# One weight pair fewer is converted in the FFT filter, and the conversions are spread differently

## The chip, the cores and the metric

The kernel runs on one core of a Trainium2 chip. The time is the device time of one execution in microseconds (us), a median of three runs. Engines: TensorE (PE, with PEld for its weight loads), VectorE (DVE), ScalarE (ACT), GpSimd (POOL), and SyncE (SP), whose queue issues every DMA of this kernel.

## The reference, cut

```python
def reference(x, filt_r, filt_i, w_in, w_out, w2_in, w2_out):        # x: 2 x 3008 x 256
    X = np.fft.rfft(x, axis=1)
    y = np.fft.irfft(X * (filt_r + 1j * filt_i)[None], n=3008, axis=1).astype(np.float32)
    t = y.reshape(6016, 256)
    h = t @ w_in                        # 256 x 2048
    t = np.maximum(0.01 * h, h) @ w_out # 2048 x 256
    h = t @ w2_in
    r = np.maximum(h, 0.0)
    return (r * r) @ w2_out
```

## The kernel before

**Filter.** The 3008 points are split as 47 x 64. The work runs in 32 units, 16 blocks of 16 channels times two batches. Iteration s of the loop (L686) has, in this order on each engine: TensorE `stage_a` (first transform of unit s, tile `pa`), `stage_b` of unit s-1 (second transform, `px`), `stage_i` of unit s-3 (back, `zps`; one product for units in `SWAP`, two for the others) and, from s = 19 on, `stage_o` (eight matmul instructions, a block `pi` of the inverse transform of the first half of the channels); VectorE a transpose of `zps` into `zin` (unit s-4), a transpose of `pa` into `bin` (unit s), the sum of two products for some units, and the product `px` times `fr`; ScalarE a copy of `px` into `xc` (two half copies for units in `SWAP`), sign rows that multiply the loaded `fi` by signs (`sign_k`, three or four columns per iteration), and the copies of `pi`; GpSimd the product of `xc` and `fi` and some of the sums. VectorE's product of a unit starts behind ScalarE's copy of that unit.

Behind the loop come 16 `fill` calls (L749): four products of the inverse transform for the second half of the channels into one of four PSUM tiles, and a copy out, on VectorE for the numbers in `OUT_V` and on ScalarE for the rest. The first fills need the transposes `zin` of all units of a batch. Between the fills stand the steps of `macro_steps`, which split the first 1024 tokens into the operands of the products.

**MLPs.** Both MLPs are done in 96 steps: a step is one weight pair (256 of the 2048 hidden columns) for one block of up to 1024 tokens. Its eight blocks of 128 x 128 x 512 are done as seven products (Strassen), and each product is three matmuls, since every fp32 operand is held as a hi part and a lo part. `up(i, part)` writes four PSUM tiles `ph0` to `ph3`, of each of which there is one; `down(i, blk)` adds the output into `py0` to `py3`. TensorE's order in a step is: the products A11 (into `ph0`) and S2 (`ph1`), two matmul groups of `down` of the step before, S1 (`ph2`), A12 (`ph0`), S3 (`ph3`), four groups of `down`, A22 (`ph1`), S4 (`ph2`), two groups of `down`. VectorE does five sums per step from PSUM: v (`ph1` and ScalarE's copy `p1`), u (`ph3` + v), and h of the blocks (1,1) (`ph2` + u), (1,0) (`ph1` + u) and (0,1) (`ph2` + v). For each of the four blocks ScalarE then applies the activation twice (`g` in fp32 and `gp` as its rounded hi part) and GpSimd takes the difference, the lo part. Since there is one `ph1`, the next step's S2 waits until h (1,0) has been read from it.

**Weights.** The weights come as pairs of words of 64-bit numbers and are turned into fp32 hi and lo parts by the kernel, a pair p in two halves k: `w_in` (0) and `w_out` (1). `narrow_w` makes the steps: `size` (ScalarE, L209), `upper` (VectorE, two instructions, L213 and L214), `signed` (L217), `exp` (L222) and `low` (L228), all VectorE; `load` (the DMA of the next pair's raw words); `add` (L236); for k = 0 `sums` (four sums of 128 x 128, L241 to L244); `hi_i`, `hi_o` (ScalarE, L269) and `lo_i`, `lo_o` (L273). `add`, `sums` and `lo` are on VectorE where `ON_VECTOR` names them for the kind of the pair, else on GpSimd. Their buffers hold one or two pairs.

**Order.** Every engine does its instructions in the order in which the code emits them. Two clocks, F and M, emit the conversion steps: `begin` enters each step with its start plus its entry in a table (`NARROW_F`, `NARROW_1`), and `tick` emits what is due. F ticks four times per iteration of the filter's loop, once per fill, and on with M. M ticks eight times a step of the MLPs (`TM`): two ticks behind v, one before and one behind the block of u and h (1,1), two in part 2, one behind h (1,0), one behind h (0,1). Tick 0 of M is the first of step 0. In the kernel before, pairs 0 to 3 start at F ticks `STARTS` = -10, 34, 72 and 112, thus about units 0, 10, 20 and 30, and pairs 4 to 7 at M ticks `STARTS_1` = 0, 32, 48 and 64. Pair 3 is first used in step 3 and pair 4 in step 8, since the first visit of the first token block has pairs 0 to 3 only.

## Time and profile before

| | |
|---|---|
| median of three runs | 1124.01 us (1123.03 to 1125.35) |
| the profiled execution | 1125.17 us, of which the span from first to last instruction is 1123.4 us |
| TensorE busy | 1106.2 us, 98% of the span |
| VectorE, ScalarE, GpSimd busy | 640.2, 659.8, 755.1 us |
| mean granted TensorE clock | 0.995 |
| filter loop | up to about 112 us |
| fills | 114.65 to 129.02 us |
| MLPs | from 129.02 us on |

In the rows below, a timeline row gives start and duration in us, engine, line, operation, result tile and source tiles, shapes, and how many instructions were put together; in brackets is how long the engine had been idle, and what released it. Tile names stand without buffer numbers. The ends of pipelined matmuls are modelled. A step of the MLPs is found in TensorE's timeline by its `ph` and `py` groups.

### The profile page before, as it was taken

The numbers are of one execution on the slowest core, as the hardware profiler recorded it, in microseconds if no ns is written. First come the engines' busy times: TensorE is split into PE (matmuls) and PEld (weight loads), VectorE is DVE, ScalarE is ACT, GpSimd is POOL, SyncE is SP. The second block draws the span as 40 slices with busy tenths as digits, with TensorE's granted clock in tenths as the row PEclk, the third lists the DMA queues.
The fourth block names the chain that finished last, engine by engine and source line by source line (L and its number), as shares of the span: only waits on it lengthen the run. The fifth ranks groups of instructions, "written<-read, shape, count | busy, mean of one in ns | idle before, by whom it ended". The sixth has DMA issues, their size and how long they took to land.

```text
span 1123.4 us, 14254 instructions
## 1 busy us (share of the span) xinstructions
PE 1106.2 (98%) x4800; PEld 883.7 (79%) x4800; DVE 640.2 (57%) x873; ACT 659.8 (59%) x1210; POOL 755.1 (67%) x612
## 2 busy tenths in 40 slices
PE   7899999999999999999999999999999999999998
PEld 4466878888888888888888888888888888888887
DVE  6799878866756746746754644434435334334332
ACT  3865566555645645645656766656656556556654
POOL 4685698876866867767768877557547547547544
PEclk8999999999999999999999999999999999999999
DMA  8644622135131221221113220200200200200100
GB/s 232 192 152 131 247 80 76 57 120 162 70 111 38 79 84 38 82 81 38 63 53 115 87 89 1 74 1 1 76 1 1 73 1 1 73 1 1 38 1 35
DMA packets 35240, 80.14 MB, mean 71 GB/s; under 512 B 4544, under 2 KB 14880, under 8 KB 35040
## 3 DMA queue, kind: packets, MB, share of 16 engines
q1 hardware_dynamic: 35168, 79.25, 21.2%
q8 instruction: 37, 0.61, 0.2%
q14 instruction: 35, 0.29, 0.1%
HBM read 51.31 MB, written 27.92 MB: 71 GB/s over the span
## 4 chain that ended last, share of the span: by engine, by line
PE 91%; DVE 3%; POOL 2%; DMA 2%; issue 2%; ACT 1%; SPq 0%; DVEq 0%; POOLq 0%; ACTq 0%
PE py L469 46%; PE ph L368 40%; PE pi L635 2%; DMA xin<-in_x 1%; PE pa L577 1%; PE px L589 1%; PE zps L619 1%; DMA fi<-in_fi 1%; POOL gp L391 0%; DVE zin L628 0%; DVE bin L584 0%; PE zps L621 0%; POOL t L607 0%; DVE t L601 0%; POOL xs L333 0%
## 5 line engine op out<-in xcount | busy, mean ns | idle before, releaser
L391 POOL TENSOR_TENSOR gp<-g,gp 128x512 fp32r<-128x512 f32 (+1 forms) x384 | 506.6, 1324 | 313.1 <-ACT gp L390 98.3
L469 PE MATMUL py<-gp,wao 128*128 128x512 f32 (+1 forms) x1152 | 287.1, 390 | 0.6 <-POOL gp L391 0.6
L469 PE MATMUL py<-gp,wbo 128*128 128x512 f32 (+1 forms) x1152 | 286.6, 391 | 0.0
L469 PEld LDWEIGHTS py<-gp,wao 128*128 128x128 f32 x1152 | 215.9, 187 | 48.6 <-POOL gp L391 1.0
L368 PE MATMUL ph<-xop,wbi 128*128 128x512 f32 (+1 forms) x1008 | 253.9, 390 | 0.0
L368 PE MATMUL ph<-xop,wai 128*128 128x512 f32 (+1 forms) x1008 | 253.8, 391 | 0.0
L469 PEld LDWEIGHTS py<-gp,wbo 128*128 128x128 f32 x1152 | 216.0, 188 | 47.8 <-POOL gp L391 0.3
L368 PEld LDWEIGHTS ph<-xop,wbi 128*128 128x128 f32 x1008 | 189.0, 187 | 41.8
L368 PEld LDWEIGHTS ph<-xop,wai 128*128 128x128 f32 x1008 | 188.9, 188 | 41.6
L402 DVE TENSOR_TENSOR u<-ph,v 128x512 f32<-128x512 f32 (+1 forms) x96 | 65.2, 680 | 176.0 <-PE ph L368 176.0
L381 ACT ACTIVATE g<-h 128x512 f32<-128x512 f32 (+1 forms) x144 | 89.4, 621 | 103.5 <-DVE h L402 102.3
L389 ACT ACTIVATE g<-h 128x512 f32<-128x512 f32 (+1 forms) x144 | 89.2, 619 | 88.2 <-DVE h L398 87.6
L402 DVE TENSOR_TENSOR v<-ph,p 128x512 f32<-128x512 f32 (+1 forms) x96 | 65.0, 678 | 120.7 <-PE ph L368 117.6
L398 DVE CUSTOM_DVE_ANT_0 h<-ph,u 128x512 f32<-128x512 f32 (+1 forms) x96 | 65.2, 680 | 84.0 <-PE ph L368 82.2
L402 DVE TENSOR_TENSOR h<-ph,u 128x512 f32<-128x512 f32 (+1 forms) x96 | 65.1, 679 | 55.0 <-PE ph L368 52.3
L422 ACT ACTIVATE p<-ph 128x512 f32<-128x512 f32 (+1 forms) x96 | 56.2, 586 | 54.8 <-PE ph L368 54.8
L382 ACT ACTIVATE gp<-h 128x512 fp32r<-128x512 f32 (+1 forms) x144 | 87.7, 609 | 0.0
L390 ACT ACTIVATE gp<-h 128x512 fp32r<-128x512 f32 (+1 forms) x144 | 87.7, 609 | 0.0
L387 ACT ACTIVATE r<-ph 128x512 f32<-128x512 f32 (+1 forms) x48 | 28.1, 586 | 68.8 <-PE ph L368 68.7
L381 ACT ACTIVATE g<-ph 128x512 f32<-128x512 f32 (+1 forms) x48 | 28.2, 587 | 59.9 <-PE ph L368 59.9
L344 DVE TENSOR_TENSOR xop<-x,xop 128x512 fp32r<-128x512 f32 (+1 forms) x33 | 49.4, 1497 | 13.4 <-ACT xop L338 7.2
L607 POOL TENSOR_TENSOR t<-xc,fi 128x384 f32<-128x384 f32 x32 | 35.4, 1111 | 24.2 <-ACT xc L597 18.1
(197 smaller groups left out, 1048.2 us busy)
## 6 DMA issues: line engine op xcount, KB each, us to landing
wraw<-in_w SPq DMA_DIRECT2D x32, 512.0 KB
xin<-in_x SPq DMA_DIRECT2D x32, 160.0 KB
xt<-xo SPq DMA_DIRECT2D x26, 188.0 KB
yt<-o SPq DMA_DIRECT2D x16, 256.0 KB
x<-yt SPq DMA_DIRECT2D x4, 1024.0 KB
out<-o SPq DMA_DIRECT2D x16, 256.0 KB
w<-wi SPq DMA_DIRECT2D x8, 448.0 KB
wi<-w SPq DMA_DIRECT2D x8, 448.0 KB
```

The costliest lines, as they stand in the source:

```text
L344: eng.tensor_tensor(t[:, 1, :n], x_f32[v][name], t[:, 0, :n].bitcast(F32), ALU.subtract)
L368: nc.tensor.matmul(ph[:, :n], w[:, i, k], x[:, j, :n], start=(first and a == 0), stop=(a == 2), skip_group_check=True)
L381: nc.scalar.activation(g[:, :n], h[:, :n], AF.Prelu, alpha=0.01)
L382: nc.scalar.activation(t[:, 0, :n], h[:, :n], AF.Prelu, alpha=0.01)
L389: nc.scalar.activation(g[:, :n], h[:, :n], AF.Square)
L390: nc.scalar.activation(t[:, 0, :n], h[:, :n], AF.Square)
L391: nc.gpsimd.tensor_tensor(t[:, 1, :n], g[:, :n], t[:, 0, :n].bitcast(F32), ALU.subtract)
L398: nc.vector._custom_dve(dve_ops.TENSOR_ADD_SAT, out=t[:, :n], in0=ph[:, :n], in1=s[:, :n], s0=F32_MAX, s1=0.0)
L402: nc.vector.tensor_tensor(t[:, :n], ph[:, :n], s[:, :n], ALU.add)
L422: nc.scalar.activation(p1[:, :n], ph[0][:, :n], AF.Copy)
L469: nc.tensor.matmul(acc[c, t][:, :n], w[:, j, 2 * f + c], g[:, k, :n], start=(p == p0 and f == t and a == 0), stop=(p == p1 - 1 and f != t ...
L607: nc.gpsimd.tensor_tensor(t2, xc, fi_of(units[s][1], units[s][1] + 1), ALU.mult)
```

## The change

Three pairs, not four, start on the F clock: pair 0 as before, with the loads of pair 1's raw words moved from ticks 23 and 35 to 46 and 58; pair 1 at F tick 64, beside units 18 to 30, with a table of its own that gives about one step per unit; pair 2 at 128, so that it begins in the loop's last two iterations and goes on beside the fills. Pair 3 starts at M tick 0, where pair 4 stood; pairs 4 to 7 start at 28, 40, 52 and 64. For all pairs on the M clock `sums` goes from GpSimd to VectorE. Of the fills' copies, seven go from VectorE to ScalarE. The second half of `fi` is loaded in two parts (in units 6 and 11 instead of all in unit 7), and its sign rows are two sets of half the size, in units 9 to 16 and 17 to 24.

```diff
--- before.py
+++ after.py
@@ -44,24 +44,24 @@
 SWAP_V = (3, 16, 17, 18, 20, 21, 25, 26, 27, 29, 30)
 
 
-FI = ((2, 4, 2), (4, 8, 2), (8, 16, 7))
+FI = ((2, 4, 2), (4, 8, 2), (8, 12, 6), (12, 16, 11))
 SGN = (1, 2)
-SIGN = ((4, 8, 4, 4), (8, 16, 9, 3))
+SIGN = ((4, 8, 4, 4), (8, 12, 9, 3), (12, 16, 17, 3))
 
 
 
 H0 = 3
 DRAIN = (2, 2, 2, 2)
 FILLS = 13
-OUT_V = (0, 1, 2, 3, 4, 5, 6, 7, 9)
+OUT_V = (0, 2)
 
 FIN = (0, 0)
 
 
 
 TM = 8
-STARTS = (-10, 34, 72, 112)
-STARTS_1 = (0, 32, 48, 64)
+STARTS = (-10, 64, 128)
+STARTS_1 = (0, 28, 40, 52, 64)
 STARTS_2 = 96
 
 
@@ -69,9 +69,19 @@
 SAVE = dict(b11=2, t2=3, t1=4, b21=5, t3=6, t4=7, b22=8)
 AGAIN = dict(b11=-30, t2=-6, t1=-5, b21=-4, t3=-4, t4=-1, b22=0)
 
-NARROW_F = dict(
-    size0=8, upper0=10, signed0=12, exp0=14, low0=15, add0=18, size1=18, upper1=20, signed1=22, load0=23, sums=23,
-    exp1=26, low1=27, hi_i=30, lo_i=31, add1=32, load1=35, hi_o=38, lo_o=39,
+NARROW_F = (
+    dict(
+        size0=8, upper0=10, signed0=12, exp0=14, low0=15, add0=18, size1=18, upper1=20, signed1=22, sums=23, exp1=26,
+        low1=27, hi_i=30, lo_i=31, add1=32, hi_o=38, lo_o=39, load0=46, load1=58,
+    ),
+    dict(
+        size0=8, upper0=10, signed0=15, exp0=19, low0=23, add0=26, load0=27, sums=28, hi_i=30, size1=30, lo_i=31,
+        upper1=33, signed1=38, exp1=42, low1=46, load1=47, add1=50, hi_o=53, lo_o=55,
+    ),
+    dict(
+        size0=8, upper0=10, signed0=14, size1=14, exp0=16, low0=18, load0=19, add0=20, upper1=22, sums=23, signed1=24,
+        exp1=26, low1=28, add1=29, load1=29, hi_i=30, lo_i=31, hi_o=32, lo_o=34,
+    ),
 )
 NARROW_1 = dict(
     size0=0, upper0=7, signed0=8, exp0=9, low0=11, load0=11, add0=11, size1=12, sums=12, upper1=15, signed1=15, exp1=15,
@@ -96,9 +106,8 @@
 ON_VECTOR = dict(
     F0=(),
     F1=("add0", "lo_o"),
-    F2=("lo_o", "add1"),
-    F3=("add0", "lo_o", "add1"),
-    N1=("add1", "lo_o"),
+    F2=("add0", "lo_o", "add1"),
+    N1=("add1", "lo_o", "sums"),
     N2=(),
     S=("lo_o",),
     M=("lo_b11", "lo_b21", "lo_t2", "lo_t3", "lo_t4"),
@@ -682,7 +691,7 @@
         n = len(units)
         h0 = w0 = 0
         for k, t in enumerate(STARTS):
-            begin("F", narrow_w(0, k, f"F{k}"), NARROW_F, t)
+            begin("F", narrow_w(0, k, f"F{k}"), NARROW_F[k], t)
         for s in range(n + 4):
             if 2 <= s < n - 3:
                 load_x(s + 3)
@@ -769,8 +778,8 @@
                 begin("M", {"load": load_part}, {"load": (NP - HALF - 2) * TM}, t)
             else:
                 begin("M", macro_steps(v, "M"), MACRO, t)
-        for p in range(NWA, NP):
-            begin("M", narrow_w(0, p, "N1"), NARROW_1, STARTS_1[p - NWA])
+        for p in range(len(STARTS), NP):
+            begin("M", narrow_w(0, p, "N1"), NARROW_1, STARTS_1[p - len(STARTS)])
         for p in range(NP):
             begin("M", narrow_w(1, p, "N2"), NARROW_2, STARTS_2 + 4 * p * TM)
             begin("M", split_w(1, p, "S", {}), SPLIT_W, ((NM - 1) * NP + p) * TM + LATE[p])
```

VectorE at the end of the loop, from the second last iterations to the transpose of unit 30 (`zin10`, from `zps0`), before:

```order
L222 TENSOR_SCALAR wi32_1019<-wb__991 128x512
L601 TENSOR_TENSOR t1_1024<-px_1007,fr_886 128x384
L228 SCALAR_TENSOR_TENSOR wm_983<-wraw0_794,wi32_1019 128x512
L628 STREAM_TRANSPOSE zin10_679<-zps1_122 128x16x16x2
L614 TENSOR_TENSOR t1_1024<-t1_1024,t2_1039 128x384
L236 TENSOR_TENSOR wi32_1019<-wb__991,wm_983 128x512
L601 TENSOR_TENSOR t1_1048<-px_1033,fr_886 128x384
L213 TENSOR_SCALAR wm_1043<-wm_1043 128x512
L214 TENSOR_SCALAR wb__1064<-wm_1043 128x512
L628 STREAM_TRANSPOSE zin11_120<-zps2_123 128x16x16x2
L217 SCALAR_TENSOR_TENSOR wb__1064<-wraw1_893,wb__1064 128x512
L628 STREAM_TRANSPOSE zin10_679<-zps0_121 128x16x16x2
```

and now:

```order
L623 TENSOR_TENSOR t1_983<-t1_983,t2_999 128x384
L610 TENSOR_TENSOR t1_1007<-px_993,fr_875 128x384
L637 STREAM_TRANSPOSE zin10_659<-zps1_122 128x16x16x2
L623 TENSOR_TENSOR t1_1007<-t1_1007,t2_1021 128x384
L610 TENSOR_TENSOR t1_1027<-px_1015,fr_875 128x384
L637 STREAM_TRANSPOSE zin11_120<-zps2_123 128x16x16x2
L637 STREAM_TRANSPOSE zin10_659<-zps0_121 128x16x16x2
```

The six conversion instructions of pair 3 among the transposes, products and sums of units 28 to 31 are gone.

VectorE in step 5 of the MLPs, from h (1,1) on to the next step's u, before (the second half of pair 5 stands behind h (0,1)):

```order
L402 TENSOR_TENSOR h_1810<-ph2_1758,u_1808 128x512
L228 SCALAR_TENSOR_TENSOR wm_1683<-wraw0_1419,wi32_1782 128x512
L402 TENSOR_TENSOR h_1842<-ph1_1757,u_1808 128x512
L402 TENSOR_TENSOR h_1852<-ph2_1758,v_1773 128x512
L213 TENSOR_SCALAR wm_1827<-wm_1827 128x512
L214 TENSOR_SCALAR wb__1854<-wm_1827 128x512
L217 SCALAR_TENSOR_TENSOR wb__1854<-wraw1_1491,wb__1854 128x512
L222 TENSOR_SCALAR wo32_1858<-wb__1854 128x512
L402 TENSOR_TENSOR v_1883<-ph1_1867,p1_1873 128x512
L228 SCALAR_TENSOR_TENSOR wm_1827<-wraw1_1491,wo32_1858 128x512
L402 TENSOR_TENSOR u_1913<-ph3_1869,v_1883 128x512
```

and now, from h (1,1) to h (0,1):

```order
L411 TENSOR_TENSOR h_1813<-ph2_1756,u_1811 128x512
L222 TENSOR_SCALAR wm_1773<-wm_1773 128x512
L223 TENSOR_SCALAR wb__1820<-wm_1773 128x512
L226 SCALAR_TENSOR_TENSOR wb__1820<-wraw1_1482,wb__1820 128x512
L231 TENSOR_SCALAR wo32_1824<-wb__1820 128x512
L237 SCALAR_TENSOR_TENSOR wm_1773<-wraw1_1482,wo32_1824 128x512
L411 TENSOR_TENSOR h_1847<-ph1_1755,u_1811 128x512
L411 TENSOR_TENSOR h_1857<-ph2_1756,v_1771 128x512
```

Five conversion instructions of pair 4's second half stand between the two h's where one of pair 5 stood. In step 6, from u to h (1,0), VectorE now has:

```order
L411 TENSOR_TENSOR u_1914<-ph3_1872,v_1886 128x512
L411 TENSOR_TENSOR h_1916<-ph2_1871,u_1914 128x512
L237 SCALAR_TENSOR_TENSOR wm_1779<-wraw0_1745,wi32_1892 128x512
L250 TENSOR_TENSOR wi32_1892<-wi32_1892 128x128
L251 TENSOR_TENSOR wi32_1892<-wi32_1892 128x128
L252 TENSOR_TENSOR wi32_1892<-wi32_1892 128x128
L253 TENSOR_TENSOR wi32_1892<-wi32_1892 128x128
L411 TENSOR_TENSOR h_1950<-ph1_1870,u_1914 128x512
```

Pair 5's `low` and its four sums stand there, which were on GpSimd in the kernel before.

GpSimd in steps 5 and 6, before (a block's difference is `gp`, `add0` is L236, pair 5's `lo_i` is L273):

```order
L391 TENSOR_TENSOR gp_1813<-g_1812,gp_1813 128x512
L236 TENSOR_TENSOR wi32_1782<-wb__1747,wm_1683 128x512
L241 TENSOR_TENSOR wi32_1782<-wi32_1782 128x128
L242 TENSOR_TENSOR wi32_1782<-wi32_1782 128x128
L243 TENSOR_TENSOR wi32_1782<-wi32_1782 128x128
L244 TENSOR_TENSOR wi32_1782<-wi32_1782 128x128
L391 TENSOR_TENSOR gp_1845<-g_1844,gp_1845 128x512
L391 TENSOR_TENSOR gp_1876<-g_1875,gp_1876 128x512
L273 TENSOR_TENSOR wbi_1885<-wi32_1782,wbi_1885 128x896
```

and now (`lo_i` is L282, `add0` is L245):

```order
L282 TENSOR_TENSOR wbi_1832<-wi32_1715,wbi_1832 128x896
L400 TENSOR_TENSOR gp_1850<-g_1849,gp_1850 128x512
L400 TENSOR_TENSOR gp_1879<-g_1878,gp_1879 128x512
L400 TENSOR_TENSOR gp_1907<-g_1906,gp_1907 128x512
L400 TENSOR_TENSOR gp_1919<-g_1918,gp_1919 128x512
L245 TENSOR_TENSOR wi32_1892<-wb__1860,wm_1779 128x512
L400 TENSOR_TENSOR gp_1953<-g_1952,gp_1953 128x512
L400 TENSOR_TENSOR gp_1984<-g_1983,gp_1984 128x512
L282 TENSOR_TENSOR wbi_1993<-wi32_1892,wbi_1993 128x896
```

The four sums have left this queue; pair 4's `lo_i`, pair 5's `add0` and pair 5's `lo_i` follow each other at distances of four and two block differences.

## Rows read from the trace of the kernel before

**Rows 1.** The page: busy time and share of the span, engine by engine.

```profile
PE 1106.2 (98%) x4800; PEld 883.7 (79%) x4800; DVE 640.2 (57%) x873; ACT 659.8 (59%) x1210; POOL 755.1 (67%) x612
```

**Rows 2.** TensorE's timeline, units 12 to 19: start us, us, engine, line, operation, operands.

```profile
41.97 1.02 PE L577 MATMUL pa<-xin,ra 94*128 94x512 f32 x2
...
45.53 1.62 PE L589 MATMUL px<-bin,cb 128*128 128x384 f32 x2 [2.53 <-DVE bin L584]
...
57.07 1.02 PE L577 MATMUL pa<-xin,ra 94*128 94x512 f32 x2
...
59.87 1.02 PE L577 MATMUL pa<-xin,ra 94*128 94x512 f32 x2
...
62.66 1.02 PE L577 MATMUL pa<-xin,ra 94*128 94x512 f32 x2
...
64.81 1.02 PE L577 MATMUL pa<-xin,ra 94*128 94x512 f32 x2
```

**Rows 3.** Timelines of ScalarE and VectorE, units 9 and 10; brackets: idle before, releaser.

```profile
36.73 1.12 ACT L573 ACTIVATE fi<-fi,sg 128x64 f32<-128x64 f32 x3
...
38.40 1.62 ACT L573 ACTIVATE fi<-fi,sg 128x128 f32<-128x128 f32 x3 [0.56 <-DMA fi<-in_fi]
...
41.62 0.56 DVE L601 TENSOR_TENSOR t<-px,fr 128x384 f32<-128x384 f32 x1 [2.81 <-ACT xc L597]
```

**Rows 4.** TensorE's timeline, unit 20 to the first fills.

```profile
67.90 1.02 PE L577 MATMUL pa<-xin,ra 94*128 94x512 f32 x2
...
84.73 0.91 PE L589 MATMUL px<-bin,cb 128*128 128x384 f32 x2 [0.37 <-DVE bin L584]
...
107.38 2.04 PE L635 MATMUL pi<-dd,zin 128*128 128x128 f32 x16
...
114.65 14.37 PE L635 MATMUL pi<-dd,zin 128*128 128x128 f32 x120 [1.48 <-DVE zin L628]
```

**Rows 5.** ScalarE's timeline, copies of the last fills.

```profile
127.64 1.95 ACT L642 ACTIVATE xo<-pi 128x376 f32<-128x376 f32 x4
```

**Rows 6.** TensorE's timeline in the MLPs, first matmuls of two steps.

```profile
188.16 1.56 PE L368 MATMUL ph<-xop,wai 128*128 128x512 f32 x6
...
198.66 1.56 PE L368 MATMUL ph<-xop,wai 128*128 128x512 f32 x6
```

**Rows 7.** VectorE's timeline, the steps between them, and conversion steps elsewhere.

```profile
45.31 0.64 DVE L217 SCALAR_TENSOR_TENSOR wb__444<-wraw,wb__444 128x512 int32<-128x512 int32 x1
...
109.87 0.68 DVE L236 TENSOR_TENSOR wi<-wb__991,wm 128x512 f32<-128x512 f32 x1
...
193.98 0.69 DVE L402 TENSOR_TENSOR h<-ph,u 128x512 f32<-128x512 f32 x1
...
194.59 1.78 DVE L236 TENSOR_TENSOR wo<-wb__1854,wm 128x512 f32<-128x512 f32 x1
...
198.00 0.68 DVE L402 TENSOR_TENSOR h<-ph,u 128x512 f32<-128x512 f32 x1
...
199.20 0.41 DVE L213 TENSOR_SCALAR wm<-wm 128x512 f32<-128x512 f32 x1
```

**Rows 8.** GpSimd's timeline in the same steps.

```profile
188.17 0.53 POOL L241 TENSOR_TENSOR wi<-wi 128x128 f32<-128x128 f32 x1
...
193.70 2.13 POOL L273 TENSOR_TENSOR wbi<-wi,wbi 128x896 fp32r<-128x896 f32 x1
```

**Rows 9.** Timelines of VectorE, GpSimd and TensorE, steps 1 to 3.

```profile
141.11 0.69 DVE L402 TENSOR_TENSOR h<-ph,u 128x512 f32<-128x512 f32 x1
...
144.44 1.30 POOL L236 TENSOR_TENSOR wi<-wb__1346,wm 128x512 f32<-128x512 f32 x1
...
145.33 1.56 PE L368 MATMUL ph<-xop,wai 128*128 128x512 f32 x6
...
158.19 1.43 PE L469 MATMUL py<-gp,wao 128*128 128x512 f32 x5 [0.56 <-POOL gp L391]
```

## The prediction

> **What bounds the kernel now.** The first view is the page: TensorE is busy in 1106 of the 1123.4 us [rows 1]. What can shrink is only the stretch in which TensorE waits, and that is the filter, the first 130 us. The second view is TensorE's timeline there. Unit 19 follows unit 18 after 2.15 us and unit 18 follows 17 after 2.79, with nothing waiting; the difference is a second inverse product, which units outside `SWAP` have. From unit 19 on, with a block of the inverse transform added, a unit takes 3.09 us (64.81 to 67.90) [rows 2, 4]. Against this pace I read where units come late: from unit 12 (41.97) to unit 16 (57.07) it is 15.1 us for four units [rows 2]. The third view tells why: ScalarE waits for the second half of `fi`, VectorE's product waits 2.81 us behind ScalarE's sign rows [rows 3], and pair 1's conversion stands between VectorE's transposes. At the end of the loop the fills' matmuls start at 114.65, held by VectorE's last transposes (1.48 us of waiting shown) [rows 4]. From there on TensorE has no wait but one of 0.56 us at 158.19 [rows 9]: in the MLPs every microsecond that TensorE is made to wait is added to the time.
>
> **What is gained in the filter.** *Units 12 to 16*: three of the four iterations have one inverse product (2.15) and one has two (2.79), together 9.3 us; it took 15.1. The change takes pair 1's conversion away from here, halves each sign row, and loads `fi`'s second half in two parts, the first of them earlier. What remains on ScalarE is two half copies and three sign rows of 0.37 (1.12 for three [rows 3]), with the copies some 2.1 us a unit, just under TensorE's 2.15. So I take the whole **-5.8 us**; if ScalarE and the two late loads cost half of it, -3. *Units 19 to 31*: three short waits go (the first is the 0.37 at 84.73 [rows 4]; with what follows each, 1.1 us in all), since pair 1 is now spread over twelve units and pair 2 starts only behind them: **-1.1**, between 0 and -1.1. *End of the loop*: between its last `bin` and the transpose that frees the fills VectorE had twelve instructions, of which six convert pair 3; now it has the filter's six alone. TensorE's queue without waits: the sixteen matmuls at 107.38 take 1.9, an inverse product 0.65, a block 0.93 and another inverse product 0.65 (3.09 less 2.15 is the block), so the fills start at 111.5 instead of 114.65 [rows 4]: **-3.1**, at worst -1.5. Together **-10.0**, bounds -4.5 and -10.0.
>
> **What the fills and step 0 pay.** The fills are 14.37 us of TensorE [rows 4]. VectorE gives up seven copies and takes ten conversion steps of pair 2 (0.41 to 0.68 each if alone [rows 7]): about two us more. ScalarE takes the seven copies, 0.49 each (1.95 for four [rows 5]), and pair 2's four sums and one difference on GpSimd run between the operands' differences. Followed in queue order, the last fills come about 0.65 us late and `p1` of step 0 about 0.85 late, since pair 2's hi part now stands ahead of it on ScalarE: **+1.5**, between 0 and +3.
>
> **What the MLPs pay.** A step takes TensorE 10.5 us (188.16 to 198.66 [rows 6]). Count from its first matmul. VectorE's h of block (1,1) starts at 5.8 and ends at 6.5 [rows 7]; h of (1,0), 0.68 us, must end before the next step's second product, at 11.2, since that product overwrites the bank that h reads (before: it ended at 198.68, and the bank was wanted at 199.36 [rows 6, 7]). So between these two h's there are **4.0 us** for other work (the short gap); between the step's last h and the next step's u some 5 to 6.8, with v in it (the long gap). Before, the short gap held at most one or two conversion steps. What a step costs there is seen at 194.59: the sum `add1`, 0.68 at 109.87, took 1.78 us, because GpSimd's difference `wbi` ran from 193.70 to 195.83; it ended 0.54 us behind it [rows 7, 8]. The instructions that read PSUM stay at 0.69 all the while.
>
> The Trainium skill, SBUF — State Buffer, section "Who interferes with whom", has the rule: a VectorE instruction with two SBUF inputs, or in a two-port mode, and a GpSimd instruction that reads SBUF contend for one shared pair of ports, and the loser blocks for the whole instruction. By that rule, the trace agrees; if they shared instead, the waits below would all be the ones "in time", some 6 us.
>
> *Pair 3* (where pair 4 stood). Its four sums go from GpSimd to VectorE, into the short gap, and need GpSimd's `add0`, which stands behind block (1,1)'s difference. h of step 1 ends at 141.80, `add0` at 145.74 [rows 9]. No row has a 128x128 sum on VectorE; 128x512 takes 0.68 and GpSimd's 128x128 0.53 [rows 7, 8], so four take 0.7 to 2.1; I take 1.0, a quarter of 0.68 each and some waiting, as VectorE's own row is the nearest. h of (1,0) then ends at 147.4; TensorE wants its bank at 146.03 (145.33 [rows 9] and three products' matmuls of 0.23): +1.4. The next step's short gap, with `add1` and `lo_o`, loses 0.4, and the old wait of 0.56 goes: **+1.2**, 0.5 to 2.5.
>
> *Pairs 4 to 7* stood 16 ticks (21 us) apart, now 12 (15.75), and pairs 4 and 6 start in the middle of a step. That puts three kinds of work into the short gap:
> - Steps 5 and 8: upper, signed, exp and low of the second half, three at 0.41 and two at 0.64, 2.5 us alone. But GpSimd has block (1,1)'s difference (1.30, as `add0`) and the pair's `lo_i` (2.13) in the same time [rows 8, 9]. Played through with what 194.59 shows: 213 ends at 7.25, 214 at 7.7, 217 at 8.3, GpSimd's difference at 9.5, 222 at 9.75, `lo_i` at 11.75, 228 at 12.3, h at 12.95 against 11.2: +1.8 if the gap begins in time. It doesn't: the four sums and a copy ahead of it make h of (1,1) end near 8.9, and the wait becomes 3.4.
> - Steps 6 and 9: low, then the four sums behind `add0`. From h of (1,1) to `add0`'s end 3.9 us (141.80 to 145.74), sums 1.0, h 0.65: 5.5 us behind h of (1,1), at 12.0 if that is in time (+0.8); at 14.4 if it comes at 8.9, as it does behind seven conversion steps in the long gap, against a bank then wanted at 11.6 (+2.8).
> - Step 7: `add1`, upper, signed, `lo_o` and exp, 2.8 us alone, two of them behind GpSimd's differences: +0.7 in time, +2.2 late.
>
> In time everywhere: 2 x 1.8 + 2 x 0.8 + 0.7 = 5.9. Late: 2 x 3.4 + 2 x 2.8 + 2.2 = **+14.6**, and some eight smaller waits of 0.4 to 0.7 that I leave out, as each is the size of one meeting of two instructions more or less. I take the late sum, because the long gap is full too: a pair is 2 x 2.5 + 2 x 0.68 + 1.0 = 7.4 us on VectorE, and with six differences, `add0` and `lo_i` GpSimd has 7 x 1.30 + 2.13 = 11.2: 18.6 us of instructions that cannot run together, in 15.75. At 16 ticks it was 6.4 + 13.8 + 4 x 0.53, 22.3 in 21, and there rows are stretched already. With the smaller waits the upper bound is 19. In it is also this: the next pair's first raw half is loaded one tick ahead of its use on ScalarE, not five, and ScalarE's next block stands behind that wait.
>
> **The sum.** -10.0 + 1.5 + 1.2 + 14.6 = +7.3 us. The profiled execution took 1125.17 us (its span of 1123.4 and 1.8 around it); the median of three is 1124.01, 1.2 below. On the median: **1131.3 us**.
>
> **Rivals.** *The conversions fit* (faster). Where VectorE's instructions mostly miss GpSimd's, the short gap needs only their lone durations, 2.5, 2.8, or 1.6 and the wait for `add0`, in 4.0. Then the MLPs lose about 1 us beside the fills' 1.5, and the time is 1124.0 - 10.0 + 2.5 = 1116.5. For it: three pairs were converted in 180 to 240 us without one TensorE wait. Against it: the 1.78 of `add1`, and sums that have to wait for GpSimd in any case. It decides as soon as the MLPs' waits stay under 8.5 us. Chance 0.27.
> *Gain and loss cancel.* The gaps begin in time, pairs 3 to 7 cost 1.2 + 5.9 and the fills 1.5: 1124.0 - 10.0 + 8.6 = 1122.6, and 1124 with one late gap. Chance 0.13.
> *The clock falls as well.* Behind the 2.53 us wait at 45.53 two matmuls of px took 1.62 us where the pair otherwise takes half of that [rows 2]: TensorE ran at its lower level, 1.2 GHz, and lost some 1.8 us until it was back. Four or five waits of that length would do this again: 1124.0 - 10.0 + 2.7 + 19 + 4 x 1.8 = 1143. Chance 0.12.
> *The filter gives less.* ScalarE's sign rows or the late loads hold units 12 to 16, -4.5 instead of -10, with the MLPs' loss as forecast: 1137. Chance 0.06.
>
> **How the numbers follow.** The forecast has 0.42, its own range is 1125 to 1140. Within 0.2% is 1121.8 to 1126.3, about what a measurement of this kernel can tell from no change. Faster by more: the first rival and a little of the second, 0.29. Same: the rest of the second and the forecast's lower edge, 0.13. Slower: 0.58. The range goes from 1117, which leaves out the lower half of the first rival, to 1141, which leaves out the upper half of the clock's: together 0.2.
>
> **What would show it.** The fills' matmuls from 104.5 us on, unit 16 at 51.3. In the MLPs TensorE waiting for VectorE's `h` at the second product of steps 2 and 6 to 10, 1 to 3.5 us each; the four sums right behind GpSimd's `add0`; `low` of pairs 4 and 6 ending half a us behind GpSimd's `lo_i`. If TensorE has no waits in 140 to 240 us, the part on the MLPs is wrong; if the fills start behind 108, that on the filter.

## The result and the profile after

The changed kernel takes 1140.21 us (median of four, 1139.27 to 1140.66) against 1124.38 for the kernel before: a ratio of 1.0141, 95% interval 1.0123 to 1.0158. That is +15.8 us where +7.3 was forecast. The profiled execution took 1140.66 us, its span is 1138.9 us: 15.5 more than that of before.

The page of after, engine by engine (answers to [rows 1]):

```profile
PE 1106.3 (97%) x4800; PEld 881.7 (77%) x4800; DVE 648.9 (57%) x886; ACT 665.1 (58%) x1241; POOL 740.9 (65%) x592
```

TensorE's work is the same to 0.1 us. All that was lost is waiting, so the account can be read from TensorE's timeline, as the time between marks that both kernels have. Of after (starts of units 12, 16, 25, 26 and 31, the fills, and then step 0), answering to [rows 2, 4]:

```profile
41.23 1.02 PE L586 MATMUL pa<-xin,ra 94*128 94x512 f32 x2
...
50.48 1.02 PE L586 MATMUL pa<-xin,ra 94*128 94x512 f32 x2
...
77.46 1.12 PE L586 MATMUL pa<-xin,ra 94*128 94x512 f32 x2 [0.55 <-ACT xo L651]
80.16 0.91 PE L598 MATMUL px<-bin,cb 128*128 128x384 f32 x2 [1.57 <-DVE bin L593]
...
82.49 1.02 PE L586 MATMUL pa<-xin,ra 94*128 94x512 f32 x2
...
97.92 1.02 PE L586 MATMUL pa<-xin,ra 94*128 94x512 f32 x2
...
106.40 13.35 PE L644 MATMUL pi<-dd,zin 128*128 128x128 f32 x112
...
121.14 4.04 PE L377 MATMUL ph<-xop,wai 128*128 128x512 f32 x15
126.40 0.96 PE L377 MATMUL ph<-xop,wai 128*128 128x512 f32 x3 [1.21 <-DVE v L411]
```

The same timeline in the MLPs of after: the first matmuls of steps 2, 4, 5, 6, 7, 8, 9, 10, 11 and 12 and most of the stops between them, answering to [rows 6, 9]:

```profile
139.86 0.86 PE L377 MATMUL ph<-xop,wai 128*128 128x512 f32 x3
...
162.92 1.56 PE L377 MATMUL ph<-xop,wai 128*128 128x512 f32 x6
...
173.42 1.67 PE L377 MATMUL ph<-xop,wai 128*128 128x512 f32 x6
...
181.94 3.07 PE L478 MATMUL py<-gp,wao 128*128 128x512 f32 x12 [2.31 <-ACT o L504]
...
187.65 0.86 PE L377 MATMUL ph<-xop,wai 128*128 128x512 f32 x3
...
199.82 0.86 PE L377 MATMUL ph<-xop,wai 128*128 128x512 f32 x3
203.30 0.97 PE L377 MATMUL ph<-xop,wai 128*128 128x512 f32 x3 [2.62 <-DVE h L411]
...
213.97 0.86 PE L377 MATMUL ph<-xop,wbi 128*128 128x512 f32 x3
216.47 0.98 PE L377 MATMUL ph<-xop,wbi 128*128 128x512 f32 x3 [1.64 <-DVE h L411]
...
226.39 0.86 PE L377 MATMUL ph<-xop,wbi 128*128 128x512 f32 x3
230.64 0.96 PE L377 MATMUL ph<-xop,wbi 128*128 128x512 f32 x3 [3.39 <-DVE h L411]
...
240.90 0.86 PE L377 MATMUL ph<-xop,wbi 128*128 128x512 f32 x3
244.38 0.96 PE L377 MATMUL ph<-xop,wbi 128*128 128x512 f32 x3 [2.61 <-DVE h L411]
...
255.05 0.87 PE L377 MATMUL ph<-xop,wbi 128*128 128x512 f32 x3
...
266.53 1.56 PE L377 MATMUL ph<-xop,wbi 128*128 128x512 f32 x6
```

Three marks of before that its rows above don't have (unit 31, steps 4 and 12):

```profile
103.00 1.02 PE L577 MATMUL pa<-xin,ra 94*128 94x512 f32 x2
...
167.16 1.56 PE L368 MATMUL ph<-xop,wai 128*128 128x512 f32 x6
...
251.16 1.56 PE L368 MATMUL ph<-xop,wbi 128*128 128x512 f32 x6
```

| stretch of TensorE | before, us | after, us | change | forecast |
|---|---|---|---|---|
| up to unit 12 | 41.97 | 41.23 | -0.74 | 0 |
| units 12 to 16 | 15.10 | 9.25 | -5.85 | -5.8 |
| units 16 to 31 | 45.93 | 47.44 | +1.51 | -1.1 |
| unit 31 to the fills | 11.65 | 8.48 | -3.17 | -3.1 |
| fills to step 2 | 30.68 | 33.46 | +2.78 | +1.5 |
| steps 2 and 3 | 21.83 | 23.06 | +1.23 | +1.2 |
| steps 4 to 11 | 84.00 | 103.61 | +19.61 | +14.6 |
| from step 12 on | 872.2 | 872.4 | +0.1 | 0 |

So in these two executions the filter gave 8.25 us, and the fills and the MLPs lost 23.6. From step 12 on nothing is changed. The first row is noise, and a part of the second may be: in the traces of the runs below whose filter is that of after, unit 12 starts between 40.42 and 42.60 us, and units 12 to 16 take 9.25 or 9.26 each time; in those of the three runs whose filter is that of before (its sums moved, and the two with its starts alone moved) units 12 to 16 take 13.93 to 14.58, not 15.10.

The largest of TensorE's waits in the whole of after, by releaser (line and tile that waited, engine and tile waited for, us, times, longest):

```profile
PE ph L377 <- DVE h L411: 14.8, 11, 3.4
```

What VectorE did in these stops stands in its timeline of after: `add1` of pair 2 and v in step 0; h (1,1) of step 5 and the last three of the five conversion steps of pair 4 in the short gap of step 5 (the first two take 0.42 and 0.43); and pair 5's first sum:

```profile
123.10 2.64 DVE L245 TENSOR_TENSOR wo<-wb__1167,wm 128x512 f32<-128x512 f32 x1
125.66 0.68 DVE L411 TENSOR_TENSOR v<-ph,p 128x512 f32<-128x512 f32 x1
...
181.74 0.69 DVE L411 TENSOR_TENSOR h<-ph,u 128x512 f32<-128x512 f32 x1
...
183.26 1.68 DVE L226 SCALAR_TENSOR_TENSOR wb__1820<-wraw,wb__1820 128x512 int32<-128x512 int32 x1
184.97 1.41 DVE L231 TENSOR_SCALAR wo<-wb__1820 128x512 int32<-128x512 int32 x1
186.41 2.49 DVE L237 SCALAR_TENSOR_TENSOR wm<-wraw,wo 128x512 f32<-128x512 uint32 x1
...
201.50 0.29 DVE L250 TENSOR_TENSOR wi<-wi 128x128 f32<-128x128 f32 x1 [3.34 <-POOL wi L245]
```

GpSimd's timeline of after at the same places (pair 2's `lo_i`, two block differences, pair 4's `lo_i`, pair 5's `add0`):

```profile
123.07 2.13 POOL L282 TENSOR_TENSOR wai<-wi,wai 128x896 fp32r<-128x896 f32 x1 [0.55 <-ACT wai L278]
...
183.00 3.10 POOL L400 TENSOR_TENSOR gp<-g,gp 128x512 fp32r<-128x512 f32 x2 [3.48 <-ACT gp L391]
186.06 2.30 POOL L282 TENSOR_TENSOR wbi<-wi,wbi 128x896 fp32r<-128x896 f32 x1
...
200.19 1.27 POOL L245 TENSOR_TENSOR wi<-wb__1860,wm 128x512 f32<-128x512 f32 x1
```

`low` (L237) ends 0.54 us behind `lo_i`, at 188.90 and 188.36; the sum begins when `add0` ends, after 3.34 us in which VectorE does nothing. The Trainium skill, SBUF — State Buffer, section "Who interferes with whom", says that, where the two engines contend, whichever comes second waits for the whole instruction of the other. The trace agrees: L231, 0.43 where GpSimd is idle, took 1.41 here (to 186.38) and ended 0.28 us behind GpSimd's second difference (186.10).

### The profile page after: what moved, and what is told of

The parts are those of the page before. It is cut to its first block, busy times and chain, and to the rows that moved or that the text cites. A ratio compares the mean times of both kernels' runs of the same rounds, so it can differ in the third digit from the quotient of the medians.

```text
span 1138.9 us, 14294 instructions
## 1 busy us (share of the span) xinstructions
PE 1106.3 (97%) x4800; PEld 881.7 (77%) x4800; DVE 648.9 (57%) x886; ACT 665.1 (58%) x1241; POOL 740.9 (65%) x592
## 4 chain that ended last, share of the span: by engine, by line
PE 85%; DVE 7%; issue 4%; POOL 2%; DMA 2%; ACT 1%; SPq 0%; POOLq 0%; ACTq 0%; DVEq 0%
PE py L478 42%; PE ph L377 37%; PE pa L586 2%; PE zps L628 1%; PE px L598 1%; PE pi L644 1%; DVE h L411 1%; DMA xin<-in_x 1%; POOL wi L245 1%; DMA wraw<-in_w 1%; DVE wm L222 0%; PE zps L630 0%; POOL gp L400 0%; DVE u L411 0%; DVE wi L231 0%
```

## The experiments

All times are medians with the kernel before run beside them (1123.9 to 1125.0 us); "changed" is the changed kernel, 1140.2, beside which the kernel before took 1124.4.

### The four sums

Changed kernel, sums of pairs 3 to 7 back on GpSimd:

```diff
-    N1=("add1", "lo_o", "sums"),
+    N1=("add1", "lo_o"),
```

> The changed kernel with the four sums of pairs 3 to 7 on GpSimd again, as before the change; starts and tables as changed. Theory (the sums hold VectorE behind GpSimd's sum add0): the waits of 1.06 in step 2, 2.62 in step 7 and 2.61 in step 10 shrink by 1 to 2 us each, but GpSimd is busy 2.1 us longer per pair and VectorE's conversion steps meet it more often: 1133 to 1138. Rival A (sums are not what hurts): 1140. Rival B (GpSimd's added 2.1 us per pair block VectorE as much, and the low parts of the activations come late): 1141 to 1146.

Measured 1130.81 (1129.51 to 1133.83): 9.4 us less, below the theory's range. Moving the sums is the largest single part of the loss. The stops of 1.06, 1.05, 2.62 and 2.61 for `h` are gone; those of 2.31, 1.64 and 3.39 are now 2.46, 2.08 and 0.84, and one of 1.21 is new. TensorE's timeline of this run (the twelve `py` matmuls took 4.46 instead of 2.96, at a mean granted clock of 0.83 in 180 to 190 us):

```profile
181.51 4.46 PE L478 MATMUL py<-gp,wao 128*128 128x512 f32 x12 [2.46 <-ACT o L504]
```

Changed kernel, `add0` on VectorE too, so that the sums don't wait for GpSimd:

```diff
-    N1=("add1", "lo_o", "sums"),
+    N1=("add0", "add1", "lo_o", "sums"),
```

> The changed kernel with add0 of pairs 3 to 7 on VectorE too, so that the four sums no longer wait for GpSimd. Theory (the sums cost 9.4 us because VectorE stands still until GpSimd has done block (1,1)'s difference and add0: 3.34 us before the first sum at 201.50, 3.33 at 242.57): these standstills go, add0 takes 0.68 on VectorE, and the time is that with the sums on GpSimd or a little less, 1129 to 1132. Rival (VectorE and GpSimd exclude each other, so VectorE's own time counts, whoever is waited for): 1137 or more.

Measured 1134.55 (1133.86 to 1135.21), between the two: 5.7 of the 9.4 us come back, and theory and rival both fall. That the 5.7 were VectorE standing still behind `add0`, and the other 3.7 its own time, is not shown: the edit also takes `add0` off GpSimd and puts its 0.68 on VectorE.

Kernel before, with only this part of the change:

```diff
-    N1=("add1", "lo_o"),
+    N1=("add1", "lo_o", "sums"),
```

> The kernel before with one part of the change alone: the four sums of pairs 4 to 7 on VectorE instead of GpSimd; their starts stay 0, 32, 48, 64. Theory (a pair with its sums on VectorE holds TensorE at three second products and two other places, as in the run with starts 16 ticks apart, where two steps took 23.97 us instead of 21): 1.5 us for pair 4, as pair 3 cost in the changed kernel, and 3.0 us for each of the pairs 5, 6 and 7: 1124 + 10.5, about 1134. Rival (the sums hurt only where five pairs are squeezed in): 1124 to 1126.

Measured 1136.41 (ratio 1.0111, 1.0094 to 1.0128): +12.3 us, as the theory had it and a little more. The sums cost some 3 us a pair with four pairs and 16 or 32 ticks between them, so this is no matter of squeezing.

### Spacing, and starts in the middle of a step

Changed kernel, starts 16 ticks apart (sums still on VectorE), and the same with the sums on GpSimd:

```diff
-STARTS_1 = (0, 28, 40, 52, 64)
+STARTS_1 = (0, 16, 32, 48, 64)
```

> The changed kernel with pairs 3 to 7 started at M ticks 0, 16, 32, 48, 64 instead of 0, 28, 40, 52, 64, so 16 ticks (two steps, 21 us) apart and each at the head of a step. Theory (the 12-tick spacing and the mid-step starts cost the 19.6 us that steps 5 to 11 lost): raw words land five ticks ahead of their use, so the 2.31 us wait of TensorE for ScalarE's copy in step 5 goes; the waits of 3.39 and 2.61 at the second product go; what is left is the wait for the four sums, about 1 us per pair, and some waits in steps 2 to 4, where pair 4 now meets the operands of the second token block: 1140.2 - 19.6 + 5 + 2, about 1128. Rival (the four sums per pair that VectorE took over cost about 4 us a pair wherever it stands): 1138 or more.

> The changed kernel with the sums of pairs 3 to 7 on GpSimd and with starts 0, 16, 32, 48, 64. With both undone, steps 7 on are those of the kernel before. Theory (the sums and the dense, mid-step starts are two separate costs): the waits in steps 7 to 11 vanish; pair 4 now meets the operands of the second token block in steps 2 to 5, and costs 3 to 6 us there: 1140.2 - 19.6 - 1.2 + 3 to 6, so 1122 to 1126. Rival (sums are all of it, the spacing none): 1130.8, like the run with the sums alone.

Measured 1144.17 and 1128.57. The first theory fell: with the sums on VectorE the wider spacing makes it slower still. Two steps then take 23.98 us instead of 21, with three stops for `h` in each pair of them (0.91, 0.57 and 0.70 us); the starts of steps 8 and 10 in that run's TensorE timeline:

```profile
222.18 0.86 PE L377 MATMUL ph<-xop,wbi 128*128 128x512 f32 x3
...
246.16 0.87 PE L377 MATMUL ph<-xop,wbi 128*128 128x512 f32 x3
```

With the sums on GpSimd too, steps 6 to 11 take 10.5 us each as before, and the loss is in steps 4 and 5, which take 30.14 us instead of 21 (161.60 to 191.74). Pair 4 now stands there beside the splitting of the second token block: ahead of step 4's second product VectorE's `low`, then two operand differences (`xop`), take 1.71, 1.78 and 1.75 us between the two h's, beside GpSimd's own. The time, 1128.6, is above the theory's 1122 to 1126: in both places tried, a pair moved into the MLPs costs more than the filter gave.

Kernel before, starts alone: all three late pairs in the middle of a step, or 12 ticks apart (one of them in the middle of a step):

```diff
-STARTS_1 = (0, 32, 48, 64)
+STARTS_1 = (0, 28, 44, 60)
```

> The kernel before with pairs 5, 6 and 7 started at M ticks 28, 44 and 60 instead of 32, 48 and 64: still 16 ticks apart, but in the middle of a step. Theory (a mid-step start puts the five steps of the second half between the two h's, where they have 4.0 us and take 5.8): 1.8 us for each, 1129 to 1130. Rival (only the closer spacing costs): 1124 to 1125.

```diff
-STARTS_1 = (0, 32, 48, 64)
+STARTS_1 = (0, 40, 52, 64)
```

> The kernel before with pairs 5, 6 and 7 at M ticks 40, 52 and 64, so 12 ticks apart as in the change, one of them in the middle of a step; the sums stay on GpSimd. Theory (the mid-step start costs 1.8, the spacing another 1 to 2 a pair, as in the changed kernel with the sums on GpSimd, where steps 7 to 9 lost 5.5): 1127 to 1130. Rival (with the sums on GpSimd and only three pairs close together the gaps suffice): 1124 to 1125.

Measured 1135.54 (ratio 1.0090, 1.0075 to 1.0105) and 1132.24 (1.0057, 1.0042 to 1.0072). The mechanism stands and its price was too low twice over. The first run, TensorE in step 6:

```profile
187.12 0.86 PE L368 MATMUL ph<-xop,wai 128*128 128x512 f32 x3
190.37 0.97 PE L368 MATMUL ph<-xop,wai 128*128 128x512 f32 x3 [2.39 <-DVE h L402]
191.17 2.41 PE L469 MATMUL py<-gp,wao 128*128 128x512 f32 x6
193.38 2.99 PE L368 MATMUL ph<-xop,wai 128*128 128x512 f32 x9
```

GpSimd and VectorE in the short gap ahead of that stop:

```profile
183.75 3.18 POOL L391 TENSOR_TENSOR gp<-g,gp 128x512 fp32r<-128x512 f32 x2
...
187.25 2.46 DVE L228 SCALAR_TENSOR_TENSOR wm<-wraw,wo 128x512 f32<-128x512 uint32 x1
```

and the granted clock there (columns: stretch, its length, TensorE busy, clock, share of DMA, GB/s):

```profile
190.00:195.00 5.00, 4.63 (x13) 0.66 0.30 105
```

The stop is 2.39, not 1.8, since GpSimd has two block differences there (3.18 us), of which I had counted one; and behind the stop TensorE ran at its lower level for a while: six `py` matmuls took 2.41 instead of 1.56, nine `ph` 2.99 instead of 2.26, so that from step 6 to step 7 it is 14.69 us (187.12 to 201.81), 4.19 too many. The second run has two such stops (2.09 and 2.00), each in a step that takes 3.8 to 3.9 us too long.

### ScalarE's wait for raw words

In after ScalarE stands 2.86 us for pair 5's raw words, with the copy of an output tile behind it that TensorE needs (its timeline of after):

```profile
180.74 0.66 ACT L218 ACTIVATE wm<-wraw 128x512 f32<-128x512 f32 x1 [2.86 <-DMA wraw<-in_w]
181.31 0.58 ACT L504 ACTIVATE o<-py 128x512 f32<-128x512 f32 x1
```

Changed kernel with this step four ticks later, and the same with the sums on GpSimd:

```diff
-    size0=0, upper0=7, signed0=8, exp0=9, low0=11, load0=11, add0=11, size1=12, sums=12, upper1=15, signed1=15, exp1=15,
+    size0=4, upper0=7, signed0=8, exp0=9, low0=11, load0=11, add0=11, size1=12, sums=12, upper1=15, signed1=15, exp1=15,
```

> The changed kernel with the first ScalarE step of pairs 3 to 7 (size0) four ticks later, so that the raw words have five ticks to land. Theory (the 2.31 and 0.76 us waits of TensorE for ScalarE's output copy in step 5 come from ScalarE waiting 2.86 us for raw words): they go, and the time is 1137; the waits of steps 6 to 11 stay. Rival (with TensorE that much earlier, VectorE's sums are late by as much at the next second product): 1139.5 to 1140.5.

> The changed kernel with the sums on GpSimd and the first ScalarE step of pairs 3 to 7 four ticks later. With the sums on VectorE the later step gave nothing, as VectorE's output copy stood behind the sums instead. Theory (with the sums gone ScalarE's 3.00 us wait for raw words is what holds TensorE 2.46 and 0.76 us in step 5): these go, 1127.5 to 1128.5. Rival (VectorE's five conversion steps then meet GpSimd's differences as they did with the sums on VectorE): 1130 or more.

Measured 1141.24 and 1132.75: no gain in the one (against 1140.2), and none in the other (against 1130.8; the two intervals overlap). The rival was right in the second and nearly so in the first (1139.5 to 1140.5). TensorE's wait of 2.31 (2.46 in the other) is gone from the traces, that of 0.76 is not; VectorE's five steps and GpSimd's differences then meet in full: with the sums on GpSimd the next second product waits 2.39, and the clock falls to 0.66 in 189 to 194 us. So ScalarE's lateness had only hidden VectorE's.

### The filter

Kernel before with the split sign rows alone:

```diff
-SIGN = ((4, 8, 4, 4), (8, 16, 9, 3))
+SIGN = ((4, 8, 4, 4), (8, 12, 9, 3), (12, 16, 17, 3))
```

(with `FI` as in the change)

> The kernel before with one part of the change alone: the second half of fi loaded in two parts and its sign rows in two sets of half the size. Theory (units 12 to 16 were late by 5.8 us through ScalarE's long sign rows and pair 1's conversion together, the 2.53 us wait being behind the product that waits for ScalarE): about half of it goes, 1121. Rival A (the sign rows alone): 1118.3. Rival B (pair 1's conversion on VectorE alone): 1124.

Measured 1126.54 (ratio 1.0021, 1.0011 to 1.0031): rival B, or slightly worse. In its trace units 12 to 16 take 13.46 us (40.56 to 54.02): 1.64 less than in before, but only 0.47 less than in the fastest of the other traces of before's filter (13.93). Unit 16 alone then takes 4.45 us, 1.65 more than in before.

Kernel before with pairs 1 and 2 later, without and with the split signs:

```diff
-STARTS = (-10, 34, 72, 112)
+STARTS = (-10, 48, 80, 112)
```

> The kernel before with pairs 1 and 2 of the filter started later, at F ticks 48 and 80 instead of 34 and 72; pair 3 stays at 112. Theory (the 5.8 us of units 12 to 16 are pair 1's first half on VectorE beside units 12 to 15, where ScalarE's sign rows make products late; the signs alone gave nothing): they go, and pairs 1 and 2 stand where TensorE has a slower pace of 3.09 us a unit; some 1 to 3 us of new waits in units 17 to 28: 1119.5 to 1121.5. Rival (three pairs in units 14 to 31 hold TensorE for as long as they do now): 1123 to 1126.

> As the kernel before with pairs 1 and 2 later, and the sign rows split in two sets. Theory (with pair 1 gone from units 12 to 16, long sign rows on ScalarE are what is left there): 0 to 2 us faster than with the later pairs alone. Rival (the second set of sign rows, in units 17 to 24, meets pair 1 there): as much slower.

Measured 1126.42 (ratio 1.0019, 1.0007 to 1.0031) and 1126.89 (1.0029, 1.0019 to 1.0039): if anything slower, so the rivals. Units 12 to 16 do take 9.35 us then (41.78 to 51.13), so it is pair 1 that held them, not the sign rows; but the time comes back at once. TensorE's timeline of the first:

```profile
51.13 1.02 PE L577 MATMUL pa<-xin,ra 94*128 94x512 f32 x2
...
54.09 0.91 PE L589 MATMUL px<-bin,cb 128*128 128x384 f32 x2 [1.94 <-DVE bin L584]
...
105.31 1.02 PE L577 MATMUL pa<-xin,ra 94*128 94x512 f32 x2
```

Another stop of 1.79 stands at 68.67, and units 16 to 31 take 54.18 us where before they took 45.93; the fills start at 117.16. In the stretch from 60 to 90 us of before VectorE is busy 28.6 of 30 us: there is no room that a later start could find.

Four pairs in the filter with pairs 1 and 2 spread as the change spreads its pair 1, pair 3 where it has its pair 2, and the MLPs as before:

```diff
-STARTS = (-10, 64, 128)
+STARTS = (-10, 36, 82, 128)
-STARTS_1 = (0, 28, 40, 52, 64)
+STARTS_1 = (0, 32, 48, 64)
```

(the long table twice, pair 0's loads at 38 and 48, sums on GpSimd)

> Four pairs in the filter again and the MLPs as in the kernel before; but pairs 1 and 2 are spread over twelve units each by the changed kernel's table (starts 36 and 82) and pair 3 starts at 128, beside the loop's end and the fills; signs and copies as in the changed kernel. Theory (the filter's gain comes from having one pair fewer; a pair costs TensorE some 6 to 8 us wherever it stands in a filter in which VectorE is busy 28.6 of 30 us): 1121 to 1125. Rival (it comes from the even spread): the loop is as fast as the changed kernel's within 3 us and the MLPs lose nothing: 1116 to 1119.

Measured 1124.91, ratio 1.0000 (0.9990 to 1.0010). The theory: the filter's gain is that of one pair fewer, not that of a better spread. In its trace (an execution of 1123.15 us) units 12 to 31 take 61.45 us (39.65 to 101.10), against 61.03 in before and 56.69 in after.

Changed kernel (sums on GpSimd) with pair 1 one unit earlier, to part its `lo_i` from the first operand sum:

```diff
-STARTS = (-10, 64, 128)
+STARTS = (-10, 60, 128)
```

> The changed kernel with the sums of pairs 3 to 7 on GpSimd and pair 1 started four F ticks (one unit) earlier. Theory (the waits of 0.55 and 1.57 us in units 23 and 24 come from pair 1's lo_i on GpSimd, 2.44 us, standing with the first operand sum, 1.26 us, ahead of two units' products, while VectorE's size limits of the second half are stretched to 1.32 and 1.11 us beside them): apart from the operand sum, lo_i costs less, and 1.0 to 1.5 us come back: 1129.3 to 1129.8. Rival (pair 1 costs this wherever it stands in the loop): 1130.8.

Measured 1132.56 against 1130.81: no gain. The stops of 0.55 and 1.57 (in iteration 25 of the loop, at the first transform of unit 25 and the second of unit 24, not in units 23 and 24 as the expectation has it) became 0.66 and 1.58 one unit earlier. What they come from is not settled beyond this: they move with pair 1.

### The fills

Changed kernel (sums on GpSimd) with seven copies back on VectorE:

```diff
-OUT_V = (0, 2)
+OUT_V = (0, 1, 2, 3, 4, 5, 6, 7, 9)
```

> The changed kernel with the sums on GpSimd and seven of the fills' copies back on VectorE, as before the change. Theory (in the fills VectorE is the late engine: add1 of pair 2 ends at 125.7 and v of step 0 behind it, which makes TensorE wait 1.21 us): VectorE takes 7 x 0.55 us more, and step 0 is late by up to that: 1130.8 + 3, about 1133 to 1135. Rival (the copies go into VectorE's gaps, and ScalarE is freed): 1129 to 1131.

Measured 1133.46 (1131.07 to 1137.64) against 1130.81 (1129.51 to 1133.83): +2.7, in the theory's range, but the four times of each overlap and so do their intervals against the kernel before (1.0063 to 1.0126; 1.0040 to 1.0072). That moving the copies was worth doing beside a pair is likely and not shown.

Kernel before with pair 3 moved to tick 128 by the change's last table, and the copies moved:

```diff
-STARTS = (-10, 34, 72, 112)
+STARTS = (-10, 34, 72, 128)
```

> The kernel before with pair 3 at F tick 128 by the table that the changed kernel has for its pair 2, and the fills' copies moved to ScalarE as in the change; everything else as before. It shows the loop's end and the fills alone. Theory: the fills start 3.1 us earlier (-3.1), and fills and steps 0 and 1 pay 2.8, as in the changed kernel: 1123.5 to 1124.5. Rival (the fills' cost in the changed kernel came from pair 3 standing behind them in the MLPs): 1121 to 1122.

Measured 1123.73, ratio 0.9987 (0.9978 to 0.9997). In its trace unit 31 to the fills is 8.49 us (-3.16) and the fills to step 2 33.44 (+2.76): the two terms of the changed kernel once more, and they cancel.

That kernel and the four-pair one with the pair's last steps behind v of step 0:

```diff
-        exp1=26, low1=28, add1=29, load1=29, hi_i=30, lo_i=31, hi_o=32, lo_o=34,
+        exp1=26, low1=28, load1=29, hi_i=33, lo_i=34, add1=36, hi_o=37, lo_o=38,
```

> The kernel with pair 3 in the fills, with that pair's last steps later: hi_i and lo_i at 33 and 34 instead of 30 and 31, add1 at 36 instead of 29, hi_o and lo_o at 37 and 38, so behind v of step 0. Theory (v waits for add1, which takes 2.63 us beside GpSimd's lo_i, and p1 stands behind hi_i): TensorE's waits of 1.20 for v and of 0.24 go, and as the pair is wanted only in step 3 nothing takes their place: 1122.0 to 1122.7. Rival (add1, now between step 0's h's, holds the next second product for as long): 1123.5 to 1124.5.

> The four-pair kernel with the even spread, with the same later steps of pair 3. Theory: 1.2 to 1.7 us less than the 1124.9 of that kernel: 1123.2 to 1123.7. Rival: 1124.5 to 1125.5.

Measured 1126.13 (ratio 1.0014, 1.0003 to 1.0024) and 1127.94 (1.0020, 1.0007 to 1.0033): both beyond their rivals' ranges. The first is slower than without (0.9978 to 0.9997 there); the second is not clear of it (0.9990 to 1.0010 there), and its profiled execution, 1123.31, is the fastest of its twelve, so its trace does not show what made the median. The wait for v is gone from both traces, so the moved steps made it. In the first two others took its place; its TensorE timeline:

```profile
134.15 2.36 PE L382 MATMUL ph<-xop,wai 128*128 128x512 f32 x9 [1.92 <-DVE h L416]
...
156.93 1.98 PE L483 MATMUL py<-gp,wao 128*128 128x512 f32 x5 [2.34 <-POOL gp L405]
```

No kernel tried is faster than the kernel before by 0.2%; the best is the one with pair 3 in the fills, by 0.13%.

## Why the prediction was wrong

**What failed.** Of the 8.2 us between the forecast and the two spans, 5.0 are the MLPs' late sum (14.6, measured 19.61), 2.6 the units 16 to 31 (-1.1, measured +1.51) and 1.3 the fills (+1.5, measured +2.78); 0.74 ahead of unit 12 goes the other way. In the MLPs the mechanism was right and the sum too small, since eight small waits were put at nothing and step 5 was priced too low; in the filter and the fills waits came that the forecast did not have.

**Right.** The sign; which engine is waited for, and at which instruction; units 12 to 16 (-5.85 for -5.8), the loop's end (-3.17 for -3.1) and pair 3 (+1.23 for +1.2). The stops at the second products of steps 2 and 6 to 10 are there, with 1.05 to 3.39 us. Not every detail held: `low` of pair 4 ends half a us behind `lo_i`, that of pair 6 does not (it runs 0.69 us alone, and `exp` ahead of it was the one held). For units 12 to 16 the reason was half wrong: the sign rows had no part in it that the runs could show, pair 1 had all. And that -5.8 was met so exactly is in part luck: against the other traces of before's filter (13.93 to 14.58) the gain is 4.7 to 5.3.

**Steps 4 to 11: +19.61 for +14.6.** Step by step, by their starts in after, beyond 10.5 us each: 3.73, 1.67, 3.65, 1.92, 4.01, 3.65 and 0.98 for steps 5 to 11. Two parts of the working were too small.

First, the "eight smaller waits of 0.4 to 0.7 that I leave out". Where the forecast had 2.8, 2.2, 3.4 and 2.8 for the late h of steps 6, 7, 8 and 9, the second products came 2.8, 1.8, 3.6 and 2.8 us late (203.30, 216.47, 230.64 and 244.38, each less its step's start and the 0.70 of one product). What is over in steps 7 to 11 is 3.3 us in smaller stops. Leaving them out, as I did, treated them as if some could be less than nothing, and nothing in the gaps could make them so.

Second, step 5 and its h: 5.4 us (3.73 and 1.67) for 3.4. The working has "GpSimd has block (1,1)'s difference (1.30, as `add0`) and the pair's `lo_i` (2.13) in the same time". There were two differences, 3.10 us in after and 3.18 with the mid-step starts alone. The working has the five steps in 5.8 us (6.5 to 12.3); they took 6.55 (182.35 to 188.90), so some 0.75 of the 2.0 missing can be the second difference's; for the rest the cause stays open. That h of (1,1) would end near 8.9 was right (9.0: 182.43 less 173.42). More than half of the 5.4 (0.76 and 2.31 us) shows up as TensorE waiting for ScalarE's output copy. The two runs without the 2.31 show that this is not a cost of its own; the 0.76 stood in them too.

The upper bound of 19 for this term, which had the smaller waits in it, was nearly met (passed by 0.6). The value inside the bounds was chosen by leaving out what could not be placed, all of it on one side.

**The share of the sums** comes out near what was measured when it is added up afterwards: 1.2 for pair 3, twice 2.8 and the 1.6 that they make each of the two five-step gaps late, 10.0 in all; taking them out gave 9.4. That makes them two thirds of what the MLPs were to pay, which the forecast, with its items by step, does not say. It is no price for other places: in the kernel before four pairs cost 12.3.

**Units 16 to 31: +1.51 for -1.1.** The step that failed is "three short waits go": they went, and pair 1 brought stops of 0.55 and 1.57 us in iteration 25. I had taken the spread over twelve units as making the steps free, in a stretch where VectorE had been idle for 1.4 us in 30. The four-pair runs bear the other view out: in the three spreads tried the pairs hold TensorE in the filter for at least as long as before.

**Fills to step 2: +2.78 for +1.5.** The fills' own 0.65 came true (14.74 us from the first fill to step 0, against 14.12). Step 0's v was to be late behind `p1`; it was late behind `add1`, which took 2.64 us beside GpSimd's `lo_i`, and ended 2.3 us behind `p1` (125.74 and 123.46). I had priced pair 2's steps "each if alone" here and had not used the exclusion that its next part, on the MLPs, rests on.

**The rivals.** That the conversions fit is refuted by eleven stops for `h`. The clock did not fall in the changed kernel's MLPs: its granted clock was 1.00 in all of them in the profiled execution, so 1140, nearer to that rival's 1143 than to the forecast, was reached without its mechanism; the three other executions, at mean clocks of 0.996 to 0.997, took no longer. "Gain and loss cancel" wanted the gaps to begin in time, with h (1,1) of step 5 ending at 6.5; it ended at 9.0. "The filter gives less" happened in part, 8.25 instead of 10.0 (0.74 of the 8.25 is the noise ahead of unit 12), but not where that rival had it: units 12 to 16 gave all that was forecast.

## What to carry over

When two engines exclude each other, add up their instructions in each gap, all of them, and take the upper end if the sum is over the gap; small meetings didn't average out here (3.3 us), since nothing gave time back on the engine that everything waits for. A chain of steps that alternates between such engines inside one gap (difference, `add0`, four sums, `h`) can cost the whole chain: here 3 us a pair for 1.1 us of instructions. And a stretch that is slowed by work on a nearly full engine was not healed here by moving the work along it: before counting the gain of a move, see whether the place it goes to is emptier.

## What the runs showed of the hardware

The same kind of stop let TensorE's clock fall in some executions and not in others. Throughout the filter the changed kernel and the one with its sums on GpSimd are the same program, and both wait 1.57 to 1.58 us in iteration 25. Granted clock behind it (columns as above), in the run with the sums on GpSimd, where it is the lower of the two levels, 1.2 GHz:

```profile
80.00:82.00 2.00, 2.00 (x4) 0.50 0.64 195
```

and in after, where it stays at 2.4 GHz, behind the longest stop of the MLPs (3.39 us) too:

```profile
80.00:82.00 2.00, 1.84 (x8) 1.00 0.60 188
230.00:239.00 9.00, 8.27 (x34) 1.00 0.16 58
```

From unit 25 to 26 it is 6.41 us in the one (76.68 to 83.09) and 5.03 in the other (77.46 to 82.49). So 1.4 us of a comparison can be the clock's, and the fall behind the 2.39 us stop above (0.66) does not follow from the stop's length alone: after stopped for 3.39 us without it. What decides it is open.
